# A delta-rule recurrence whose steps are split into single-engine operations and listed in one hand-made order, with the solved blocks on four column quarters

## Chip, cores, metric

One core of one Trainium2 chip runs the whole program in one launch. The metric is device time in microseconds (us), the median over executions. Matrix products run on TensorE (PE in the profile; its weight loads are PEld), elementwise work on VectorE (DVE), ScalarE (ACT) and GpSimd (POOL), and all transfers are issued by SyncE (SP). Every engine takes its own instructions strictly in the order in which the built program lists them, and waits on semaphores where an input is not there yet.

## What is computed

The program has three stages: a recurrence over 768 time steps for 4 x 8 = 32 heads of size 40, a mixture of attention experts, and a mixer with two pairs of dense layers. The change touches the first stage alone:

```python
for t in range(S):                       # S = 768
    y[:, :, t] = einsum('bhd,bhde->bhe', rt, state)
    Sa = einsum('bhde,bhe->bhd', state, at)
    state_decay = state * wt[:, :, None, :] - einsum('bhd,bhe->bhde', Sa, bt)
    state = state_decay + einsum('bhd,bhe->bhde', vt, kt)
x = moe2(moe(y))
```

## The kernel before

**Chunks and pairs.** The 768 steps are 12 chunks of 64 steps, and two chunks (128 steps) form a pair, of which there are 6. The 32 heads of 40 channels lie on partitions in 11 groups of three heads (120 rows; the last group has two). Three head ranges, `QUADS`, take 4, 4 and 3 groups, and are called q = 0, 1, 2 below: 12, 12 and 8 heads.

**What a pair needs ahead of its chunks.** Its inputs come by DMA: w, a and kb (k and b together) per pair, v, r and small strided copies of a and r (tiles `abd` and `rbd`, one buffer each) per chunk. `decay` makes running products of w on DVE, 31 dependent multiplications of 120x88, then four normalizing operations. `scale` multiplies a and kb by them. `scores` makes, per chunk, six masked products of kb and abd (PE, then DVE into tile `sc`), and copies 32x32 diagonal blocks of it to tile `td` (ACT). `solve` then inverts 128 x 32 small triangular systems on DVE: one transposition to `tp`, 31 steps of a product `pr` and a subtraction from `x`, and a transposition to `xt`. Each `x` needs the `pr` ahead of it, and each `pr` the `x` ahead of it.

**The chain of a chunk**, for each q: `z1` (state times a, PE), `tv` (scores times v and u, PE) and a copy to `zt` (ACT, with the sign turned), `xz` (the solved block `xt` times `zt`, PE), a copy to `vu` (ACT); then `tv` and `xz` again for the second 32 steps; `ds` (PE) and a product with `mf` into the new state `ST` (DVE); `st` transposes it to `S` (PE, ACT). The chunk's outputs follow at leisure: `vut`, `rs`, `hh`, `yy`. The first `xz` of a pair needs that pair's `xt`, so pair p cannot go on before `solve(p)` ended.

**Column halves.** `tv`, `xz`, `hh` and `yy` put two heads side by side into column halves of the PE array (`sides`): heads of groups g0 and g0+1 in one half, the others in the other, which makes 6 + 6 heads in q = 0 and 1, and 6 + 2 in q = 2. The copies of `zt` and `vu` take 32 partitions each: 240 columns twice, or 240 and 80 (`spans`).

**What sets the order.** Two strings, `EVEN` and `ODD`, name a chunk's operations in the order in which they are written, and `pump(1)` puts one step of the solve or of the decay (a list in the background, taken one by one) behind each. A scheduler of the framework then orders the instructions of every engine by its own model, and interleaves what it finds ready. The second and third stage are written after the recurrence and scheduled with it.

Of the kernel before, what the change touches and what calls it, by code (L numbers as in the profile page):

```python
# [31 lines left out]
FIRST = "p0 S p1 p2 k0 k1 k2 X L D M V q0 q1 q2"  # L32
SPIN = 28
PN = (1, 1)
EVEN = "m2 v0 h0 c0 z0 v1 c1 r0 c2 D v2 z2 x2 c3 m0 c4 x0 t2 z1 y0 x1 t1 c5 t0 h1 r1 r2 x3 y1 h2 c6 c7 k0 x5 c8 s0 c9 y2 x4 c10 c11 s2 d0 m1 S L d2 s1 k1 k2 d1"
ODD = "A z0 x0 v0 v1 z1 z2 r0 h0 x2 t0 m1 x1 m2 s0 v2 r1 y0 h1 m0 r2 M y1 p0 L p1 p2 h2 y2 x3 t1 t2 d0 s2 k0 x5 s1 k1 x4 d2 k2 d1"
QUADS = [(0, 4), (4, 8), (8, 11)]

def sides(q, n):

    g0, g1 = QUADS[q]
    a, b, e = n * g0, n * (g0 + 2), min(n * g1, 32 if n > 1 else G)
    for i in range(b - a):
# [26 lines left out]
class Rec:  # L70
# [39 lines left out]
    def load_w(s, p):  # L110
        w = s.ek.tile([120, G, 2, 64], F32, name="w", bufs=1)
        s.nc.sync.dma_start(w.rearrange("p g c t -> p g (c t)"), s.in_w[p])
        s.T[p] = dict(w=w)

    def load_a(s, p):
        a = s.wk.tile([120, G, 2, 64], F32, name="a")
        s.nc.sync.dma_start(a.rearrange("p g c t -> p g (c t)"), s.in_a[p])
        s.T[p]["a"] = a

    def load_kb(s, p):  # L120
        kb = s.ek.tile([120, G, 2, 128], F32, name="kb")
        s.nc.sync.dma_start(kb, s.in_kb[p].rearrange("p g c x t -> p g c (x t)"))
        s.T[p]["kb"] = kb
# [23 lines left out]
    def decay(s, p):  # L147
# [46 lines left out]
    def scores(s, c, u):  # L194

        nc, t = s.nc, s.T[c // 2]
        if u == 0:
            s.T["sc", c] = s.wk.tile([128, 32, 64], F32, name="sc", bufs=4)
        sc, abd = s.T["sc", c], s.T["abd", c]
        gs = range(2 * u, min(2 * u + 2, G))  # L200
        ps = s.ps.tile([128, 6, 64], F32, name="psc")
        n = 0
        for g in gs:
            k = 40 * nheads(g)
            nc.tensor.matmul(ps[:, n:n + nheads(g), :], t["kb"][:k, g, c % 2, :],  # L205
                             abd[:k, g, :nheads(g), :], start=True, stop=True)
            n += nheads(g)
        sv = sc[:, 6 * u:6 * u + n, :]
        m = s.mask[:, None, :].to_broadcast([128, n, 64])
        nc.vector.tensor_tensor(sv, ps[:, :n, :], m, OP.mult)  # L210
        if u == 5:

            if c % 2 == 0:
                s.T["td", c // 2] = s.ek.tile([128, 32, 32], F32, name="td", bufs=1)
            td = s.T["td", c // 2]
            for h in range(2):
                q = 64 * (1 - c % 2) + 32 * h
                nc.scalar.activation(td[q:q + 32],
                                     sc[q:q + 32, :, 32 * h:32 * h + 32], AF.Copy)

    def solve(s, p):
# [3 lines left out]
        yield  # L225
# [14 lines left out]
        s.solved = v.transpose(xt.rearrange("p s t -> p t s"), x)  # L240
        s.T["xt", p] = xt

    def kbt(s, c, q):
        nc, t = s.nc, s.T[c // 2]
        if q == 0:
            s.T["kbt", c] = s.wk.tile([128, 1280], F32, name="kbt")
# [3 lines left out]
        for g in range(g0, g1):  # L250
            k = 40 * nheads(g)
            nc.tensor.transpose(ps[:, o:o + k], t["kb"][:k, g, c % 2, :], s.ident[:k, :k])
            o += k
        nc.scalar.activation(s.T["kbt", c][:, 120 * g0:120 * g0 + o], ps[:, :o], AF.Copy)

    def ptt(s, p, q):
        nc, t = s.nc, s.T[p]
        if q == 0:
            s.T["ptt", p] = s.wk.tile([128, 1280], F32, name="ptt", bufs=3)
        g0, g1 = QUADS[q]  # L260
        ps = s.ps.tile([128, 512], F32, name="pm")
        o = 0
        for g in range(g0, g1):
            k = 40 * nheads(g)
            nc.tensor.transpose(ps[:, o:o + k], t["pt"][:k, g].rearrange("p c t -> p (c t)"), s.ident[:k, :k])
            o += k
        nc.scalar.activation(s.T["ptt", p][:, 120 * g0:120 * g0 + o], ps[:, :o], AF.Copy)


    def z1(s, c, q):  # L270
        nc, t = s.nc, s.T[c // 2]
        zu = s.pz.tile([128, 480], F32, name="zu")
        s.T["zu", q] = zu
        for g, b, i in sides(q, 1):
            k = 40 * nheads(g)
            nc.tensor.matmul(zu[64 * b:64 * b + 64, 120 * i:120 * i + k], t["a"][:k, g, c % 2, :],  # L276
                             s.ST[:k, g, :k], start=(i == 0), stop=False, skip_group_check=True)
        s.tv(c, q, 0)

    def tv(s, c, q, half):  # L280

        nc = s.nc
        zu, sc, vu = s.T["zu", q], s.T["sc", c], s.T["vu", c]
# [3 lines left out]
        for h, b, i in sides(q, 3):  # L287
# [864 lines left out]
```

## Time and profile before

| | us |
|---|---|
| median of 3 executions (1044.83 to 1048.39) | 1047.39 |
| the profiled execution, device time | 1045.46 |
| its span, first to last instruction | 1043.7 |
| PE busy (92%) | 959.1 |
| DVE busy (65%) | 674.4 |
| ACT busy (46%) | 479.3 |

The profile is of one execution. Busy time counts an instruction from its start to its end, and PE's overlap in its pipeline, so a busy PE can still lose time between two matmuls: the distance from start to start shows that. Other engines' instructions can overlap by a little as well. PEclk is the TensorE clock that was granted, as a share of 2.4 GHz. One f32 matmul of the program stands as two records in the trace.

### The profile page before, as it was taken

Reading aid. Unit: us, or ns where it says so; the run is one execution under the profiler, and the core shown is the slowest. Engines: PE = TensorE matmul, PEld = TensorE weight load, DVE = VectorE, ACT = ScalarE, POOL = GpSimd, SP = SyncE. Lnnn points to the kernel's source line nnn. Section 1 sums busy time; section 2 is a strip of 40 time slices with the busy share of each in tenths; the row PEclk is TensorE's granted clock in tenths of the full one; section 3 lists DMA queues with packets and bytes.
Section 4 is the critical chain, followed back from the end, with each engine's and each line's share of the span. In section 5 each row is a group of like instructions: output and inputs, shape, how many; then the busy total and the mean of one; then the engine's idle time right before and its main releaser. Section 6 shows DMA issues by size and latency. Waiting matters only on the chain.

```text
span 1043.7 us, 23515 instructions
## 1 busy us (share of the span) xinstructions
PE 959.1 (92%) x9313; PEld 823.1 (79%) x9313; DVE 674.4 (65%) x1793; ACT 479.3 (46%) x1250; POOL 167.7 (16%) x214
## 2 busy tenths in 40 slices
PE   2977997999999999966999999999998999999998
PEld 1646876888888898855877888888787898898987
DVE  6598898887989685747898777566287222222222
ACT  1324544656665665534677667666543121121211
POOL 5000000010000000352234132223255000000000
PEclk9977996999999999979999999999999999999999
DMA  8604422417253323455543441420262101101000
GB/s 172 138 1 96 100 67 74 111 41 170 53 123 74 86 61 117 157 165 145 154 116 99 118 115 31 96 65 26 87 205 63 56 1 56 39 18 57 1 26 26
DMA packets 101031, 88.84 MB, mean 85 GB/s; under 512 B 60785, under 2 KB 91073, under 8 KB 100321
## 3 DMA queue, kind: packets, MB, share of 16 engines
q1 hardware_dynamic: 100921, 87.34, 32.2%
q8 instruction: 74, 1.21, 0.5%
q14 instruction: 36, 0.29, 0.1%
HBM read 54.94 MB, written 15.73 MB: 68 GB/s over the span
## 4 chain that ended last, share of the span: by engine, by line
PE 66%; DVE 19%; DMA 6%; ACT 4%; issue 3%; POOL 1%; SPq 1%; DVEq 0%; ACTq 0%; POOLq 0%
PE pq L1045 12%; PE p L1059 11%; PE psc L205 4%; PE zu L289 3%; PE psc L387 3%; DVE pq L164 3%; PE po L872 3%; PE pq L846 3%; PE zu L302 2%; PE pq L998 2%; PE pm L325 2%; PE zu L276 2%; DVE x L237 2%; PE y L400 2%; DVE pr L235 2%
## 5 line engine op out<-in xcount | busy, mean ns | idle before, releaser
L1049 DVE SCALAR_TENSOR_TENSOR hl<-pq,hh 128x512 fp32r<-128x512 f32 x72 | 49.7, 690 | 153.6 <-ACT hh L1048 153.6
L1048 ACT ACTIVATE hh<-pq 128x512 fp32r<-128x512 f32 x72 | 42.9, 596 | 186.7 <-PE pq L1045 186.7
L1059 PE MATMUL p<-c2h,hh 128*128 128x320 f32 x288 | 90.8, 315 | 0.0
L819 ACT ACTIVATE a<-s,nm 128x512 f32<-128x512 f32 (+3 forms) x128 | 68.7, 542 | 46.4 <-DVE nm L816 21.6
L1059 PE MATMUL p<-c2l,hh 128*128 128x320 f32 x288 | 89.4, 311 | 0.2 <-POOL c2l L635 0.2
L1059 PE MATMUL p<-c2h,hl 128*128 128x320 f32 x288 | 89.5, 311 | 0.1
L306 ACT ACTIVATE vu<-zu 32x240 f32<-32x240 f32 (+1 forms) x144 | 48.8, 339 | 55.2 <-PE zu L302 45.1
L293 ACT ACTIVATE zt<-zu 32x240 f32<-32x240 f32 (+1 forms) x144 | 48.7, 338 | 51.7 <-PE zu L289 49.6
L814 DVE TENSOR_REDUCE nm<-s 128x1 f32<-128x512 f32 (+3 forms) x128 | 62.0, 500 | 15.7 <-PE s L813 10.8
L164 DVE TENSOR_TENSOR pq<-w,pq 120x88 f32<-120x88 f32 x186 | 61.2, 329 | 9.7 <-DMA w<-in_w 5.8
L832 POOL TENSOR_TENSOR a<-a,rs 128x128 f32<-128x128 f32 (+1 forms) x64 | 45.6, 734 | 126.6 <-DVE rs L827 84.5
L235 DVE TENSOR_TENSOR pr<-tp,x 128x31 f32<-128x31 f32 (+15 forms) x186 | 63.0, 339 | 3.8 <-DVE tp L226 0.5
L237 DVE TENSOR_TENSOR x<-x,pr 128x31 f32<-128x31 f32 (+15 forms) x186 | 63.2, 340 | 3.3
L289 PE MATMUL zu<-vu,sc 64*32 64x40 f32 (+1 forms) x1536 | 61.3, 220 | 1.2 <-ACT vu L306 1.2
L302 PE MATMUL zu<-zt,xt 64*32 64x40 f32 x1536 | 48.3, 211 | 12.5 <-DVE pq L161 6.8
L1045 PE MATMUL pq<-uh,c1h 128*128 128x512 f32 x144 | 57.6, 400 | 0.8 <-DVE ul L666 0.8
L289 PEld LDWEIGHTS zu<-vu,sc 64*32 64x32 f32 (+1 forms) x1536 | 53.2, 127 | 6.2 <-ACT vu L306 2.9
L1059 PEld LDWEIGHTS p<-c2h,hh 128*128 128x128 f32 x288 | 54.5, 189 | 3.7 <-DVE o L1062 1.2
L1045 PE MATMUL pq<-uh,c1l 128*128 128x512 f32 x144 | 57.1, 396 | 0.0
L1059 PEld LDWEIGHTS p<-c2l,hh 128*128 128x128 f32 x288 | 54.5, 189 | 2.9 <-POOL c2l L635 0.5
L387 PE MATMUL psc<-rbd,vut 120*128 120x192 f32 (+1 forms) x264 | 54.6, 341 | 1.9 <-DVE sr L391 1.6
L302 PEld LDWEIGHTS zu<-zt,xt 64*32 64x32 f32 x1536 | 40.3, 117 | 20.1 <-issue 12.8
(206 smaller groups left out, 2504.4 us busy)
## 6 DMA issues: line engine op xcount, KB each, us to landing
kb<-in_kb SPq DMA_DIRECT2D x5, 1320.0 KB
kh<-hb SPq DMA_DIRECT2D x64, 96.0 KB
cv<-in_c SPq DMA_DIRECT2D x18, 256.0 KB
w<-in_w SPq DMA_DIRECT2D x6, 660.0 KB
a<-in_a SPq DMA_DIRECT2D x6, 660.0 KB
r<-in_r SPq DMA_DIRECT2D x12, 330.0 KB
rbd<-in_r SPq DMA_DIRECT2D x36, 110.0 KB
vu<-in_v SPq DMA_DIRECT2D x12, 320.0 KB
```

Source lines behind the costliest of these rows:

```text
L164: e.tensor_tensor(two(pq, i + 1, x + 29 - 2 * i), two(t["w"], i, 31 - 2 * i), two(pq, i, x + 31 - 2 * i), OP.mult)
L235: v.tensor_tensor(prv, tp[:, j + 1:, j:j + 1].to_broadcast([128, n, j + 1]), x[:, j:j + 1, :j + 1].to_broadcast([128, n, j + 1]), OP.mult)
L237: v.tensor_tensor(x[:, j + 1:, :j + 1], x[:, j + 1:, :j + 1], prv, OP.subtract)
L289: nc.tensor.matmul(zu[o:o + m, 40 * i:40 * i + 40], sc[r, h, 32 * half:32 * half + m], vu[r, 40 * h:40 * h + 40], start=False, stop=True, ...
L302: nc.tensor.matmul(zu[o:o + 32, 240 + 40 * i:280 + 40 * i], xt[r, h, :], s.zt[half][r, 40 * h:40 * h + 40], start=True, stop=True, skip_gr ...
L306: nc.scalar.activation(vu[d:d + 32, o:o + n], zu[b + 32 * half:b + 32 * half + 32, 240:240 + n], AF.Copy)
L387: nc.tensor.matmul(ps[:, n:n + nheads(g), :], vt[:k, g - g0, :], rbd[:k, g, :nheads(g), :], start=True, stop=True)
L814: nc.vector.tensor_reduce(nm[:, x:x + 1], s, axis=AX.X, op=OP.max, negate=True)
L819: nc.scalar.activation(a[:, n0:n1], s, AF.Exp, bias=nm[:, -1:] if nb_ == 2 else nm[:, :1], accum_out=sm[:, x, i % 2:i % 2 + 1])
L1045: nc.tensor.matmul(p, l, r, start=(n == 0), stop=(n == 7))
L1049: nc.vector.scalar_tensor_tensor(hl, p, 0.0, hh, op0=OP.max, op1=OP.subtract)
L1059: nc.tensor.matmul(Y[s][i], hs[x][:, ts], w[:, k], start=(k + n == 0), stop=(k == 11 and n == 2))
```

## The change

Every operation of the recurrence is split into the part of one engine: lower-case letters of a list name a PE part or a DMA, capital letters the copy or product that empties it (`scores` and `scores_out`, `xz` and `xz_out`, and so on). Solve and decay are generators that yield after each single DVE instruction. Two lists, `HEAD` (up to the first `xt`) and `PAIR` (run once for each pair, with numbers relative to it), give the order, and `tc.manual_schedule` makes each engine keep it.

The solve works in `tp` itself, without `x`: 30 steps, each one column narrower, and -1 is written on the diagonal before the transposition, so that `xt` is the negative and the copy to `zt` needs no sign. `xz` puts its heads on four column quarters of 32, by contiguous quarters of the heads (3 each, or 2 in q = 2), with a place of its own for each half in the `zu` tile, and its copy is four pieces of 120 (or 80) columns. `sides`, `spans` and the new `blocks` split the heads evenly in all q: 6 + 6, 6 + 6, 4 + 4; group 9 of `z1` and `hh` becomes two matmuls for that.

```diff
+PAIR = """
+K-1.2 G0 N1.3 G0 G0 r-2.2.0 r-2.2.1 S-1.0 p1.2 F1 x-1.0.1 G0 P1.2 p1.0 j2 P1.0 R-2.2.1 p1.1 h-2.1 G0 y-2.1
...
+c3.0 Y-1.1 x0.0.0 R-1.2.0 E2 Z0.1 E2 E2 x0.2.0 S0.0 x0.1.0 C3.0 h-1.2 y-1.2 X0.0.0 X0.2.0 E2 c3.1 t0.0 C3.1 i0
...
+"""
...
+def sides(q):
+    g0, g1 = QUADS[q]
+    n = (min(3 * g1, 32) - 3 * g0) // 2
+    for i in range(n):
+        yield 3 * g0 + i, 0, i
+        yield 3 * g0 + n + i, 1, i
...
-        x = s.ek.tile([128, 32, 32], F32, name="x", bufs=1)
-        nc.gpsimd.memset(x, 0.0)
-        nc.gpsimd.memset(x.rearrange("p a b -> p (a b)")[:, ::33], 1.0)
-        for j in range(31):
+        for j in range(1, 31):
             n = 31 - j
             yield
             pr = s.ek.tile([128, 256], F32, name="pr")
-            prv = pr[:, :n * (j + 1)].rearrange("p (t c) -> p t c", c=j + 1)
-            v.tensor_tensor(prv, tp[:, j + 1:, j:j + 1].to_broadcast([128, n, j + 1]),
-                            x[:, j:j + 1, :j + 1].to_broadcast([128, n, j + 1]), OP.mult)
-            v.tensor_tensor(x[:, j + 1:, :j + 1], x[:, j + 1:, :j + 1], prv, OP.subtract)
+            prv = pr[:, :n * j].rearrange("p (t c) -> p t c", c=j)
+            v.tensor_tensor(prv, tp[:, j + 1:, j:j + 1].to_broadcast([128, n, j]),
+                            tp[:, j:j + 1, :j].to_broadcast([128, n, j]), OP.mult)
+            yield
+            v.tensor_tensor(tp[:, j + 1:, :j], tp[:, j + 1:, :j], prv, OP.subtract)
         yield
+        v.memset(tp.rearrange("p a b -> p (a b)")[:, ::33], -1.0)
...
-        for h, b, i in sides(q, 3):
-            o = 64 * b + 32 * half
-            nc.tensor.matmul(zu[o:o + 32, 240 + 40 * i:280 + 40 * i], xt[r, h, :],
-                             s.zt[half][r, 40 * h:40 * h + 40], start=True, stop=True, skip_group_check=True)
+        n = (min(3 * g1, 32) - 3 * g0) // 4
+        o = 240 + 120 * half
+        for i in range(n):
+            for b in range(4):
+                h = 3 * g0 + n * b + i
+                nc.tensor.matmul(zu[32 * b:32 * b + 32, o + 40 * i:o + 40 * i + 40], xt[r, h, :],
+                                 s.zt[half][r, 40 * h:40 * h + 40], start=False, stop=True, skip_group_check=True)
...
+        for b in range(4):
+            p = 40 * (3 * g0 + n * b)
+            nc.scalar.activation(vu[d:d + 32, p:p + 40 * n], zu[32 * b:32 * b + 32, o:o + 40 * n], AF.Copy)
...
+        with s.tc.manual_schedule(engines={E.PE, E.Activation, E.DVE, E.Pool, E.SP}):
+            for o in HEAD.split():
+                step(o, 0)
+            done.update(("E1", "G0"))
+            for i in range(s.np + 2):
+                for o in PAIR.split():
+                    step(o, i)
```

On DVE, before, these are the first steps of the solve of pair 0 and of pair 3 (L235 is `pr`, L237 `x`, L333 the product into `ST`, L226 the transposition from `td`):

```order
L226 STREAM_TRANSPOSE tp<-td 128x1024
L235 TENSOR_TENSOR pr<-tp,x 128x31
L237 TENSOR_TENSOR x<-x,pr 128x31
L235 TENSOR_TENSOR pr<-tp,x 128x60
L237 TENSOR_TENSOR x<-x,pr 128x30x2
L235 TENSOR_TENSOR pr<-tp,x 128x87
L237 TENSOR_TENSOR x<-x,pr 128x29x3
L235 TENSOR_TENSOR pr<-tp,x 128x112
L333 TENSOR_TENSOR ST<-pm,mf 120x480
L237 TENSOR_TENSOR x<-x,pr 128x28x4
```

And now, the first steps of the solve of pair 1 (L272 is the transposition, L278 `pr`, L281 the subtraction, L195 a decay step of pair 2, L246 a masked product, L395 the product into `ST`):

```order
L395 TENSOR_TENSOR ST<-pm,mf 120x480
L272 STREAM_TRANSPOSE tp<-td 128x1024
L278 TENSOR_TENSOR pr<-tp 128x30
L195 TENSOR_TENSOR pq<-w,pq 120x2x44
L281 TENSOR_TENSOR tp<-tp,pr 128x30
L278 TENSOR_TENSOR pr<-tp 128x58
L195 TENSOR_TENSOR pq<-w,pq 120x2x44
L281 TENSOR_TENSOR tp<-tp,pr 128x29x2
L195 TENSOR_TENSOR pq<-w,pq 120x2x44
L278 TENSOR_TENSOR pr<-tp 128x84
L281 TENSOR_TENSOR tp<-tp,pr 128x28x3
L246 TENSOR_TENSOR sr<-psc,mask 128x384
```

Between an instruction and the one that needs its result another stands now in most places. From the first transposition to the last `xt`, DVE has 791 instructions before and 788 now, and pairs of neighbours of which the second needs the first are 275 before and 157 now.

On PE, before, the stretch around the first `xz` of pair 3 reads so (L342 is `st`, L302 `xz`, L289 `tv`, L387 `rs`, L400 `yy`, L205 `scores`, L357 `hh`):

```order
L342 MATMUL pm<-ident,ST 120x120 x3
L302 MATMUL zu<-zt_113,xt 32x40 x21
L289 MATMUL zu<-vu,sc 32x40 x8
L302 MATMUL zu<-zt_113,xt 32x40 x11
L289 MATMUL zu<-vu,sc 32x40 x12
L387 MATMUL psc<-rbd,vut 128x192 x2
L289 MATMUL zu<-vu,sc 32x40 x12
L387 MATMUL psc<-rbd,vut 128x128
L302 MATMUL zu<-zt_114,xt 32x40 x12
L400 MATMUL y<-kbt,sr 64x40 x12
L205 MATMUL psc<-abd,kb 128x192 x4
L357 MATMUL y<-S,r 64x120
```

And now, at the same place of pairs 1 to 3 (L241 is `scores` and `rs`, L353 `xz`, L415 `hh`, L449 `yy`, L334 `tv`):

```order
L241 MATMUL psc<-abd,kb 128x192 x2
L353 MATMUL zu<-zt_113,xt 32x40 x32
L415 MATMUL y<-S,r 64x120
L415 MATMUL y<-S,r 64x80
L415 MATMUL y<-S,r 64x40
L415 MATMUL y<-S,r 64x80
L449 MATMUL y<-kbt,sr 64x40 x8
L241 MATMUL psc<-abd,kb 128x192 x2
L334 MATMUL zu<-vu,sc 32x40 x12
L241 MATMUL psc<-abd,kb 128x192 x4
L353 MATMUL zu<-zt_113,xt 32x40 x12
L241 MATMUL psc<-abd,kb 128x192 x2
```

An operation's matmuls stand together more often. Over the recurrence, neighbours on PE that use the array in different shapes (whole, column halves, or 64 rows by 32 columns) are 305 before and 183 now, and the matmuls are 3180 and 3193. In the two later stages the instructions are the same, but the scheduler lists some of them in another order: 1464 of 3442 PE instructions stand elsewhere.

On SP, in the list, the loads of a and kb of the next pair but one stand one behind the other, with the small copies `abd` behind them:

```order
L170 DMA r<-in_r 120x11x64
L151 DMA a<-in_a 120x1408
L156 DMA kb<-in_kb 120x2816
L234 DMA abd<-a 40x11x64 x3
L178 DMA rbd<-in_r 40x11x64 x3
```

The load of a waits for the last `z1` of the pair's odd chunk, and that of kb for its last turned kb (`kbt`), both on PE.

## Rows read from the trace of the kernel before

**Rows 1.** Windows: us, then busy time of each engine, clock, DMA share.

```profile
core 0: us, PE busy (x) PEld busy (x) DVE busy (x) ACT busy (x) POOL busy (x), PEclk, DMA share, GB/s
43.80:397.90 354.10, 324.12 (x4815) 275.14 (x4813) 306.52 (x791) 190.04 (x500) 17.93 (x29) 0.94 0.34 81
71.60:166.10 94.50, 78.82 (x1033) 67.17 (x1033) 86.23 (x233) 45.41 (x110) 4.58 (x10) 0.86 0.34 82
166.10:397.90 231.80, 224.13 (x3714) 198.56 (x3714) 195.16 (x497) 143.32 (x385) 13.35 (x19) 0.97 0.36 86
397.90:446.20 48.30, 45.88 (x831) 38.93 (x831) 29.23 (x61) 24.98 (x65) 13.59 (x10) 1.00 0.48 148
446.20:1043.70 597.50, 565.02 (x3527) 489.88 (x3527) 315.39 (x887) 251.82 (x662) 120.61 (x146) 0.98 0.28 77
```

**Rows 2.** Timeline of DVE: solves that begin and end, the last product into ST.

```profile
43.83 1.99 DVE L226 STREAM_TRANSPOSE tp<-td 128x1024 f32<-128x1024 f32 x1 [2.19 <-ACT td L218]
...
69.73 1.90 DVE L240 STREAM_TRANSPOSE xt<-x 128x1024 f32<-128x1024 f32 x1
...
395.97 1.96 DVE L240 STREAM_TRANSPOSE xt<-x 128x1024 f32<-128x1024 f32 x1
...
409.14 1.32 DVE L333 TENSOR_TENSOR ST<-pm,mf 120x480 f32<-120x480 f32 x3 [1.59 <-PE pm L327]
```

**Rows 3.** Waits between 43 and 440 us: total, times, longest.

```profile
DVE sr L391 <- PE psc L387: 17.0, 14, 5.1
```

**Rows 4.** Groups by shape, 30 to 430 us: busy, mean ns, idle before.

```profile
L164 DVE TENSOR_TENSOR pq<-w,pq 120x88 f32<-120x88 f32 x155 | 51.3, 331 | 2.8
...
L306 ACT ACTIVATE vu<-zu 32x240 f32<-32x240 f32 x117 | 42.2, 360 | 54.2 <-PE zu L302 44.4 <-issue 8.3
...
L306 ACT ACTIVATE vu<-zu 32x80 f32<-32x80 f32 x23 | 5.3, 229 | 0.3
...
L237 DVE TENSOR_TENSOR x<-x,pr 128x255 f32<-128x255 f32 x12 | 5.0, 416 | 0.1
...
L237 DVE TENSOR_TENSOR x<-x,pr 128x31 f32<-128x31 f32 x12 | 2.4, 200 | 0.3
```

**Rows 5.** Timeline of DVE: solve steps by themselves, then with others between.

```profile
46.57 0.21 DVE L237 TENSOR_TENSOR x<-x,pr 128x31 f32<-128x31 f32 x1
46.81 0.22 DVE L235 TENSOR_TENSOR pr<-tp,x 128x60 f32<-128x60 f32 x1
...
127.76 0.33 DVE L164 TENSOR_TENSOR pq<-w,pq 120x88 f32<-120x88 f32 x1
128.00 0.25 DVE L237 TENSOR_TENSOR x<-x,pr 128x87 f32<-128x87 f32 x1
```

**Rows 6.** Timeline of PE: groups in one array shape, and at a change.

```profile
184.19 0.85 PE L289 MATMUL zu<-vu,sc 128*64 128x40 f32 x24
184.86 0.50 PE L276 MATMUL zu<-ST,a 120*64 120x120 f32 x5
...
195.46 0.62 PE L302 MATMUL zu<-zt,xt 64*32 64x40 f32 x24
195.91 1.02 PE L289 MATMUL zu<-vu,sc 64*32 64x40 f32 x40
...
242.94 0.62 PE L302 MATMUL zu<-zt,xt 64*32 64x40 f32 x24
243.50 0.65 PE L367 MATMUL pm<-ident,vu 128*120 128x128 f32 x4
```

**Rows 7.** Timelines of SP and DVE: loads of kb, a, and their use.

```profile
179.40 0.33 SPq L122 DMA_DIRECT2D kb<-in_kb  x1
185.50 0.34 SPq L117 DMA_DIRECT2D a<-in_a  x1
...
188.32 1.63 DVE L186 TENSOR_TENSOR kb<-kb,pq 120x1408 f32<-120x1408 f32 x1 [2.35 <-DMA kb<-in_kb]
...
191.42 1.62 DVE L182 TENSOR_TENSOR a<-a,pq 120x1408 f32<-120x1408 f32 x1 [0.21 <-issue]
```

More of the change, by code (lines that the diff above doesn't have):

```diff
@@ L192, in abd_load, with product @@
             nc.sync.dma_start(abd[40 * h:40 * h + 40, :, h, :], a[40 * h:40 * h + 40, :, c % 2, :])
[L194 to L200, printed above, removed]
+    def product(s, w, mov, gs):
         ps = s.ps.tile([128, 6, 64], F32, name="psc")
@@ new lines, in xz_out, with mf @@
+    def xz_out(s, c, q, half):
+        nc, zu, vu = s.nc, s.T["zu", c, q], s.T["vu", c]
+        g0, g1 = QUADS[q]
+        n = (min(3 * g1, 32) - 3 * g0) // 4
+        o = 240 + 120 * half
+        d = 64 * (1 - c % 2) + 32 * half
+        for b in range(4):
+            p = 40 * (3 * g0 + n * b)
+            nc.scalar.activation(vu[d:d + 32, p:p + 40 * n], zu[32 * b:32 * b + 32, o:o + 40 * n], AF.Copy)
+    def mf(s, c, q):
+        g0, g1 = QUADS[q]
+        f = s.T[(c + 1) // 2]["f"][:, (c + 1) % 2]
+        s.T["mf", c, q] = mf = s.wk.tile([120, 4, 120], F32, name="mf", bufs=3)
+        for g in range(g0, g1):
+            s.nc.scalar.activation(mf[:, g - g0], s.bdm, AF.Copy, scale=f[:, g:g + 1])
@@ L432, in first @@
         s.consts()
-        s.bg = [s.decay(0)]
-        s.pump(1000)
+        for _ in s.decay(0):
+            pass
+        for i in range(4):
+            s.norm(0, i)
+        s.decayed(0)
         t = s.T[0]
@@ L448, in first, with advance @@
                 s.scores(c, u)
+                s.scores_out(c, u)
+            s.blocks_out(c)
+    def advance(s, f, p):
+        if (f, p) not in s.T:
+            s.T[f, p] = f(p)
+        next(s.T[f, p])
     def run(s):
-        n = s.np
         s.first()
-        def loads():
-            s.load_w(1)
-            s.load_a(1)
-            s.load_kb(1)
-        def all(f):
-            for _ in f:
-                pass
-        def decay():
-            with s.tc.issue_after(s.solved.ins):
-                all(s.decay(1))
@@ L467, in run @@
-        do = dict(S=lambda: all(s.solve(0)), p=lambda q: s.ptt(0, q), L=loads, D=decay,
-                  M=lambda: s.scale(1), q=lambda q: s.ptt(1, q), V=lambda: s.load_chunk(1),
-                  k=lambda q: s.kbt(0, q), X=lambda: s.spin(s.T['sc', 1], SPIN))
-        for o in FIRST.split():
-            if n > 1 or o[0] not in "LDMq":
-                do[o[0]](*map(int, o[1:]))
-        s.bg = []
-        for c in range(2 * n):
-            s.chunk(c)
+        by_pair = dict(W=s.load_w, I=s.load_a, J=s.load_kb, E=lambda p: s.advance(s.decay, p), N=s.norm, F=s.decayed,
+                       A=s.scale_a, B=s.scale_kb, G=lambda p: s.advance(s.solve, p), p=s.ptt, P=s.ptt_out, O=s.store,
+                       a=lambda p: s.spin(s.T["sc", 1], SPIN))
@@ new lines, in run, with step @@
+        done = set(HEAD_DONE.split())
+        skip = {f"{k}{2 * s.np - 1}.{q}" for k in "mdD" for q in range(3)} | {f"{k}0.{q}" for k in "sS" for q in range(3)}
+        def step(o, i):
+            k, (x, *rest) = o[0], map(int, o[1:].split("."))
+            one = k in by_pair
+            x += i if one else 2 * i
+            if k in "EG" and f"{k}{x}" in done:
+                return
+            name = ".".join([f"{k}{x}", *map(str, rest)])
+            if 0 <= x < (s.np if one else 2 * s.np) and name not in done and name not in skip:
+                (by_pair if one else by_chunk)[k](x, *rest)
+                if k not in "EG":
+                    done.add(name)
```

374 lines of the change are left out of this document (159 added, 215 removed).

## The prediction, made before the result was known

> **What bounds the kernel now.** I first cut the span by the solves, since a pair cannot go on before its `xt`. The first transposition starts at 43.83 us, the first `xt` ends at 71.6 and the last at 397.9 [rows 2]; the recurrence ends at 446.2, and the two later stages take 597.5 [rows 1]. So 354.1 us lie between the first solve's start and the last one's end, and there two engines are near their limit at once: PE is busy for 324.1 and DVE for 306.5, while ACT has 190.0 [rows 1]. The reader should see how unevenly the time goes: from the first `xt` to the second it takes 94.5 us at a granted clock of 0.86 of 2.4 GHz, and the other four pairs take 231.8, or 58.0 each [rows 1]. In those four PE is idle for 7.7 us and DVE for 36.6. DVE's idle time over all of the 354.1 is 47.6. The view of waits shows what it mostly is: DVE has a masked product to make and PE has not delivered it (17.0 us in 14 waits) [rows 3]. DVE is late, PE then waits for the solve, and later DVE waits for PE: each loses time that the other lacks. After the last `xt` it takes 48.3 us to the end of the recurrence [rows 1].
>
> **DVE's work.** One instruction of the solve takes 0.200 us with 31 columns and 0.416 with 255 [rows 4], so 0.170 plus 0.00096 a column. A solve had 31 steps of two instructions and 5456 columns each way; now it has 30 steps and 4960. That is 992 columns and two instructions less, 0.95 + 0.34 = 1.3 us a pair. The new write of the diagonal has no row; it has 32 columns, and the shortest solve instruction, with 31, is 0.200, so it costs between 0 and 0.2, and I take 0.1, a middle, since it only writes. Six solves save 7.2.
>
> The order saves more. Where the next instruction needs the result, it starts after the end: `x` takes 0.21 and the next `pr` starts 0.24 behind its start. Where it does not, it starts earlier than the end: a decay step takes 0.33 and the solve step behind it starts after 0.24 [rows 5]. That is 0.03 of a gap against 0.09 of overlap. The order lists 275 neighbours of the first kind before and 157 now, so 118 change kind: 10.6 us less busy time, and the gaps shrink from 275 x 0.03 = 8.3 to 4.7. Not every independent neighbour overlaps, above all where PSUM is read, so this is an upper bound; the lower one is nothing, and I take it whole, because the 118 are nearly all solve and decay steps, whose rows these are. DVE then needs 306.5 - 7.2 - 10.6 + 4.7 = 293.4 us from the first transposition to the last `xt`.
>
> In this the decay of pair 1 (31 x 0.331 = 10.3 [rows 4]), its normalizing and its scaling (3 x 1.62 [rows 7]) move from behind the first `xt` to within the first solve. They fill the solve's gaps: of 17 or so, 38 neighbours give back 0.12 each and the 38 new instructions overlap by 0.09, so the first `xt` comes some 8 us later, near 79, and what stood behind it is gone from the next 94.5 us.
>
> **PE's work.** In the four later pairs PE has 224.1 / 4 = 56.0 us of work each [rows 1]. Three things make it less:
> - Changes of the array's shape. The 24 records of an `xz` take 0.45 us to the next start where the next group has the same shape (195.46 to 195.91), and 0.56 where it has not (242.94 to 243.50) [rows 6]: 0.11 a change. 122 fewer changes are 13.4 us in all, 2.2 a pair.
> - `xz` on quarters. Those 24 records are 12 heads on two halves, 37.5 ns for each two. In q = 2 one half held six heads, so it took 12 x 37.5 ns = 0.45 too, and a half-chunk 1.35. If four quarters run as two halves do, it takes 0.225 + 0.225 + 0.15 = 0.60; if only two ever run at once, 0.45 + 0.45 + 0.30 = 1.20. Over 24 half-chunks this saves 18.0 or 3.6. No row shows four at once; I take 18.0, because the rows show two as independent of each other.
> - Even halves in q = 2. `tv`'s first half takes 0.67 for 24 records on two halves [rows 6], 56 ns for each two; two heads of two records less on the long side are 0.22, the same for `yy`, and 2 x 2 x 37.5 ns = 0.15 for `tv`'s second half. 0.59 a chunk, 7.1 in all. The one matmul more in `z1` and `hh` balances columns in the same way, and I set it at nothing: 160 columns on a side instead of 240 and 80.
>
> PE needs 56.0 - 2.2 - 3.0 - 1.2 = 49.6 us a pair, against DVE's 293.4 less some 35 for the first solve, over five pairs: 51.7. DVE leads, narrowly.
>
> **ACT.** The copies of `vu` become four pieces. With 0.360 for 240 columns and 0.229 for 80 [rows 4], 120 columns take 0.262: 1.05 in place of 0.72 for a set, 72 sets, 24 us more. ACT has 164 us to spare in the 354.1, and the pieces of one q lie beside PE's products for the next, so I count nothing; if that cover were gone it would be the 24.
>
> **What DVE still waits for.** From the end of an `xt`, the chain of `xz`, `tv`, `xz` and `ds` brings the first product into `ST` 11.2 us later (397.9 to 409.14 [rows 2]); the list puts that product ahead of the next solve, with about 25 instructions between, at a mean of 306.5 / 791 = 0.39 less overlap some 9 us. 1 to 2.5 us are left, 1.8 x 4 = 7. The loads: a was in use 5.9 us after its issue (185.50 to 191.42) and kb 8.9 us (179.40 to 188.32, DVE had waited 2.35) [rows 7]. The list issues both together behind the odd chunk's `z1`, some 5 us ahead of a's use: 1 a pair, 4. At the start one `abd` buffer has to be loaded again between the two chunks' scores, and the first `xz` stands behind it on PE: 4.5. For PE and DVE so near each other I add 3. Sum 18.5, against 47.6 - 8.3 = 39.3 before.
>
> **The sum.** Last `xt` at 43.8 + 293.4 + 18.5 = 355.7. The tail was 48.3; two chunks save 2 x (0.59 + 1.5) = 4.2, so 44.1. The recurrence ends at 399.8 in place of 446.2, 46.4 earlier. The later stages keep their instructions; some are listed in another order, which I bound by a third of PE's 32.5 us of idle time there [rows 1], 10 either way, and take at nothing. The profiled execution's 1045.46 becomes 999.1; the median before is 1.9 above it, so I predict **1001 us**.
>
> **The rivals.**
> - *Quarters do not run four at once.* PE needs 2.4 more a pair, 52.0, and is level with DVE; the chain behind `xt` grows by 0.5. Up to 14.4 come back, of which I count 9: 1010. For it: nothing in the rows shows four. Against: two halves share the same 64 rows already, at no loss. The Trainium skill (TensorE: Matmul & The Clock Gate, Wait — 56ns, not 53.3ns?) gives about 25 ns as the least distance from one matmul's start to the next, which would forbid any gain; this trace is already below it, 0.45 us / 24 = 19 ns a record [rows 6].
> - *The waits stay.* The list was fixed ahead, as the scheduler's was, and neither engine can leave its order when the other is late. If DVE waits 39.3 as before, the last `xt` is at 376.5 and the program at 1022. For it: both engines would be within 5% of their limit. Against: the large waits before come with `EVEN`, which asks for the next pair's scores only late in a chunk.
> - *The copies lie on the path.* The 24 us of ACT come back: 1025. For it: the second `tv` and `ds` need these copies. Against: ACT is idle for nearly half of the stretch [rows 1]. The Trainium skill (TensorEngine Tiling (Array Packing), PSUM Bottleneck) says that packing speeds up TensorE and not the emptying of PSUM, which may become the bottleneck behind it; no row here shows ACT as one.
> - *No change*: the waits come to 65 us, 13 a pair, 1047.
> - *Slower: the loads.* a, kb and behind them `abd` go one after the other on SP's queue. If kb lands some 15 us late, as it would if both loads took twice the 14.8 us of the rows, every solve step and score behind the scaling is late by that, 12 net of cover, in five pairs: 60 more, 1061. It decides from 46.4 / 5 = 9.3 us a pair. Against: the DMA queues are busy for a third of the time [rows 1], and kb waited only 2.35 here.
>
> **How the numbers follow.** The forecast has a chance of 0.55 and its own range is 987 to 1014: the later stages' 10 either way, and waits from 14 to 22. Quarters without effect 0.15, waits as before 0.18, copies 0.04, no change 0.04, loads 0.04. 0.3% is about what a measurement of this kernel can tell from no change. The time is lower by more than that in the first four cases, 0.92. For 8 in 10 the range takes in the second and third case with their own spread: 982 to 1030.
>
> **What would show it.** Last `xt` near 356 and the first near 79; the time from one `xt` to the next near 55 in the middle pairs and no first one of 94.5; DVE's busy time from the first transposition to the last `xt` near 289; an `xz` group of 24 records at about 0.23 us to the next of its shape. It is wrong if DVE's waits for PE stay near 40 us, if those 24 records still take 0.45, or if `a` and `kb` become DVE's largest wait.

## The result, and the profile after

The changed kernel takes 992.24 us, the median of four executions (988.11 to 998.65), against 1046.2 for the kernel before in the same series: a ratio of 0.9488 with a 95% interval of 0.9429 to 0.9546. It is faster, by 54 us where 46 were forecast. In a later series it took 991.83 (0.9487, 0.9458 to 0.9516). The profiled execution took 988.11, with a span of 986.4. (Of one experiment below, the arithmetic without the order, some executions were disturbed; its ratio leaves them out.)

The same windows as in [rows 1], cut at the first transposition, the first and the last `xt` and the end of the recurrence:

```profile
40.80:76.20 35.40, 26.12 (x97) 13.45 (x95) 34.53 (x103) 4.41 (x12) 1.55 (x3) 0.90 0.10 23
76.20:140.00 63.80, 60.38 (x1019) 53.83 (x1019) 56.82 (x158) 45.67 (x131) 2.65 (x4) 0.95 0.46 95
140.00:346.80 206.80, 202.56 (x3829) 181.05 (x3829) 195.12 (x529) 161.65 (x487) 9.17 (x13) 1.00 0.47 105
40.80:346.80 306.00, 289.06 (x4944) 248.33 (x4943) 286.47 (x788) 211.73 (x630) 13.37 (x20) 0.98 0.43 94
346.80:391.00 44.20, 39.88 (x807) 35.14 (x805) 31.04 (x59) 29.23 (x92) 14.56 (x11) 0.92 0.57 169
391.00:986.40 595.40, 566.55 (x3527) 492.14 (x3527) 313.04 (x887) 250.94 (x659) 119.59 (x145) 0.97 0.27 77
```

The stretch from the first transposition to the last `xt` fell from 354.1 to 306.0 us. That is 48.1 of the 57.3 between the two spans; 3.0 lie ahead of it, 4.1 in the tail, 2.1 in the later stages. DVE's busy time in the stretch fell by 20.0 (306.5 to 286.5) and its idle time by 28.1 (47.6 to 19.5). By place, the part up to the second `xt` fell from 122.3 us (43.8 to 166.1) to 99.2 and the four intervals behind it from 231.8 to 206.8: 23.1 and 25.0 us. The reader should also see the third row: in the last four intervals PE is busy for 202.6 of 206.8 us and DVE for 195.1, so both are near their limit. DVE was busy there for 195.2 before as well; what is gone is its idle time, 36.6 us then and 11.7 now.

DVE's timeline, as in [rows 2], and its waits in the stretch (total, times, longest), as in [rows 3]:

```profile
40.81 1.99 DVE L272 STREAM_TRANSPOSE tp<-td 128x1024 f32<-128x1024 f32 x1 [2.19 <-ACT td L266]
...
74.30 1.93 DVE L285 STREAM_TRANSPOSE xt<-tp 128x1024 f32<-128x1024 f32 x1
...
344.84 2.00 DVE L285 STREAM_TRANSPOSE xt<-tp 128x1024 f32<-128x1024 f32 x1
...
355.08 0.66 DVE L395 TENSOR_TENSOR ST<-pm,mf 120x480 f32<-120x480 f32 x1 [1.17 <-PE pm L383]
```

```profile
DVE sc L246 <- PE psc L241: 8.9, 13, 1.3
DVE tp L272 <- ACT td L266: 2.2, 1, 2.2
DVE ST L395 <- PE pm L383: 1.6, 2, 1.1
DVE sr L246 <- PE psc L241: 1.3, 2, 1.1
DVE ptt L456 <- PE y L449: 0.2, 1, 0.2
```

For comparison, DVE's waits for PE before, within the same stretch (43.8 to 397.9 us):

```profile
DVE sc L210 <- PE psc L205: 9.0, 16, 2.3
DVE sr L391 <- PE psc L387: 8.6, 9, 3.0
DVE ST L333 <- PE pm L327: 7.2, 6, 3.6
DVE ptt L404 <- PE y L400: 4.3, 10, 0.9
```

These four were 29.1 us and are 12.0 now (the 2.2 for `tp` lie ahead of the first transposition, outside the stretch); the wait for `sr` went from 8.6 to 1.3. (The 17.0 for `sr` in [rows 3] runs on to 440 us, beyond the last `xt`.) The chain from the end of an `xt` to the first product into `ST` takes 8.2 us (346.84 to 355.08) where it took 11.2.

PE's timeline, as in [rows 6]: an `xz` ahead of a group of another shape, and one ahead of its own shape.

```profile
155.94 0.42 PE L353 MATMUL zu<-zt,xt 64*32 64x40 f32 x24
156.28 0.90 PE L449 MATMUL y<-kbt,sr 128*64 128x40 f32 x24
...
160.00 0.58 PE L353 MATMUL zu<-zt,xt 64*32 64x40 f32 x40
160.39 0.62 PE L334 MATMUL zu<-vu,sc 64*32 64x40 f32 x24
```

40 records take 0.39 us to the next start, 9.75 ns each, where 24 on halves took 0.45, 18.8 each. Four quarters do run at once. 24 records ahead of another shape take 0.34, by this 0.23 and 0.11 for the change of shape. The four copies on ACT, by shape in the stretch, as in [rows 4]:

```profile
L364 ACT ACTIVATE vu<-zu 32x120 f32<-32x120 f32 x160 | 41.8, 261 | 8.5 <-PE zu L353 5.8
...
L364 ACT ACTIVATE vu<-zu 32x80 f32<-32x80 f32 x80 | 18.2, 228 | 6.0 <-PE zu L353 4.9
```

### The profile page after: what moved, and what is told of

Read it like the earlier page. It is cut to its first block, busy times and chain, and to the rows that moved or that the text cites. A ratio compares the mean times of both kernels' runs of the same rounds, so it can differ in the third digit from the quotient of the medians.

```text
span 986.4 us, 23682 instructions
## 1 busy us (share of the span) xinstructions
PE 914.2 (93%) x9350; PEld 790.6 (80%) x9350; DVE 653.8 (66%) x1787; ACT 500.5 (51%) x1390; POOL 161.0 (16%) x202
## 4 chain that ended last, share of the span: by engine, by line
PE 64%; DVE 22%; DMA 5%; ACT 4%; issue 3%; SPq 1%; POOL 0%; DVEq 0%; ACTq 0%; POOLq 0%
PE pq L1023 12%; PE p L1037 12%; PE psc L241 8%; PE po L850 4%; DVE pq L195 3%; PE pq L824 3%; DVE pr L278 2%; DVE tp L281 2%; PE pq L989 2%; PE pq L976 2%; PE pq L752 2%; PE s L788 2%; PE pq L865 2%; PE zu L334 2%; PE y L449 2%
## 5 line engine op out<-in xcount | busy, mean ns | idle before, releaser
L364 ACT ACTIVATE vu<-zu 32x120 f32<-32x120 f32 (+1 forms) x288 | 72.0, 250 | 17.2 <-PE zu L353 12.7
L195 DVE TENSOR_TENSOR pq<-w,pq 120x88 f32<-120x88 f32 x186 | 61.1, 329 | 8.0 <-DMA w<-in_w 5.6
L241 PE MATMUL psc<-abd,kb 120*128 120x192 f32 (+1 forms) x242 | 53.9, 364 | 7.2 <-DMA abd<-a 3.8
L281 DVE TENSOR_TENSOR tp<-tp,pr 128x30 f32<-128x30 f32 (+9 forms) x180 | 58.6, 326 | 2.1
L278 DVE TENSOR_TENSOR pr<-tp 128x30 f32<-128x30 f32 (+9 forms) x180 | 58.5, 325 | 1.8
L1023 PE MATMUL pq<-uh,c1h 128*128 128x512 f32 x144 | 57.1, 396 | 0.8 <-DVE ul L644 0.8
L341 ACT ACTIVATE zt<-zu 32x240 f32<-32x240 f32 (+1 forms) x144 | 49.0, 340 | 14.4 <-PE zu L334 12.3
L1037 PEld LDWEIGHTS p<-c2h,hl 128*128 128x128 f32 x288 | 54.5, 189 | 0.3 <-DVE hl L1027 0.3
L241 PE MATMUL psc<-rbd,vut 120*128 120x192 f32 (+1 forms) x264 | 53.5, 333 | 0.0
L241 PEld LDWEIGHTS psc<-abd,kb 120*128 120x128 f32 (+1 forms) x242 | 42.5, 208 | 12.7 <-DVE kb L228 3.4
L824 PE MATMUL pq<-ident,a 128*128 128x128 f32 x336 | 50.4, 276 | 1.4 <-DVE kz L762 0.6
```

Source lines behind the costliest of these rows:

```text
L241: s.nc.tensor.matmul(ps[:, n:n + nheads(g), :], w(g)[:k], mov[:k, g, :nheads(g), :], start=True, stop=True)
L281: v.tensor_tensor(tp[:, j + 1:, :j], tp[:, j + 1:, :j], prv, OP.subtract)
L364: nc.scalar.activation(vu[d:d + 32, p:p + 40 * n], zu[32 * b:32 * b + 32, o:o + 40 * n], AF.Copy)
L824: nc.tensor.transpose(p[:, o:o + 128], es[i][:, 128 * (j0 + j):128 * (j0 + j) + 128], ident)
L1023: nc.tensor.matmul(p, l, r, start=(n == 0), stop=(n == 7))
L1037: nc.tensor.matmul(Y[s][i], hs[x][:, ts], w[:, k], start=(k + n == 0), stop=(k == 11 and n == 2))
```

## The experiments

My theory was the prediction's: DVE and PE are both near their limit, the list lets neither wait, and each edit then counts. The first rivals were that the arithmetic alone does it, or the order alone. Each figure is a median in its own series, with the ratio to the kernel before in that series and its 95% interval. The diffs are against the changed kernel unless said otherwise.

**The order without the arithmetic.** The solve goes back into a tile `x`, `xz` onto two halves with two copies, q = 2 to 6 + 2 heads:

```diff
-        for j in range(1, 31):
+        for j in range(31):
...
-        for i in range(n):
-            for b in range(4):
...
+        for h, b, i in sides(q):
...
-    n = (min(3 * g1, 32) - 3 * g0) // 2
+    n, e = 6, min(3 * g1, 32) - 3 * g0
```

> The changed kernel with its lists and split operations, but the old arithmetic: the solve in a tile of its own with 31 steps, xz on two column halves with two copies, and 6 + 2 last heads. My theory (DVE and PE are level, so work given back to either shows): DVE gets 7.2 us more, PE about 21 in five pairs and 4 in the tail, ACT 24 less; the last xt comes near 365 and the whole takes 1010 to 1018, so the order alone is worth some 30 us. Rival, the order is nearly the whole gain: 1000 or less. Rival, the arithmetic carries it: 1030 or more.

Measured 1010.99 us (0.9687, 0.9658 to 0.9716); the last `xt` ended at 365.2. As expected: the order alone is worth some 33 us.

**The arithmetic without the order.** The same three edits the other way round, put into the kernel before:

```diff
-        for j in range(31):
+        for j in range(1, 31):
...
-        for h, b, i in sides(q, 3):
-            o = 64 * b + 32 * half
...
+        for i in range(n):
+            for b in range(4):
+                h = 3 * g0 + n * b + i
```

> The kernel before with its own order, but the new arithmetic: the solve in place, xz on four quarters with four copies, 4 + 4 last heads. My theory: DVE saves 7.2 us and PE up to 25, but the large waits of DVE for PE's products come with the old lists and mostly stay (over 25 us of DVE waits between the first transposition and the last xt), so 1020 to 1035. Rival, the arithmetic carries the gain: 1005 or less, with DVE waits near 15. Rival, the old order hides it all: within 5 us of the kernel before.

Measured: a ratio of 0.9998 (0.9955 to 1.0042), so no gain. My 1020 to 1035 was too good, and the rival "the old order hides it all" holds. The ratio is over executions of 1035.48 to 1047.67; the profiled one was the quickest, at a mean granted clock of 0.962, the others at 0.952 to 0.954. Even there the stretch is no more than 3.9 us shorter than before. Its window, and DVE's largest waits:

```profile
39.50:389.70 350.20, 313.47 (x4835) 261.10 (x4833) 295.89 (x783) 209.32 (x618) 12.32 (x19) 0.92 0.34 81
```

```profile
DVE ST L348 <- PE pm L342: 15.9, 11, 6.3
DVE sc L223 <- PE psc L218: 12.2, 17, 4.1
DVE sr L406 <- PE psc L402: 6.0, 13, 1.8
```

DVE is busy 10.6 us less than before and PE 10.7, but DVE is idle for 54.3 instead of 47.6 and PE for 36.7 instead of 30.0: of what either engine saves, 6.7 us go into its own idle time, and DVE's three largest waits, 34.1 us, are all for PE.

**The list given to the scheduler.**

```diff
-        with s.tc.manual_schedule(engines={E.PE, E.Activation, E.DVE, E.Pool, E.SP}):
+        with nullcontext():
```

> The changed kernel with the same split operations written in the same order, but each engine's order left to the framework's scheduler, as in the kernel before: 229 changes of the array's shape instead of 183, and 265 solve and decay neighbours that need each other instead of 166. My theory (the list itself is worth most of what the arithmetic alone did not give): DVE's waits for PE come back, 20 to 40 us, with 12 for the neighbours and 5 for the shapes: 1015 to 1045. Rival, splitting the operations is what helps and the scheduler does as well with them: within 8 us of the changed kernel.

Measured 1026.13 us (0.9796, 0.9742 to 0.9849), some 34 more than with the list. Two rows show it:

```profile
0.00:53.90 53.90, 27.73 (x173) 21.91 (x174) 39.42 (x95) 13.37 (x27) 15.04 (x30) 0.84 0.71 144
53.90:381.40 327.50, 298.86 (x4847) 255.92 (x4845) 281.82 (x750) 208.91 (x614) 11.99 (x17) 0.94 0.37 85
```

The scheduler puts pair 1's decay, normalizing and scaling ahead of the first solve, whose transposition starts 13 us later, at 53.9; and in the stretch DVE is idle for 45.7 us, as before. Of the 34 us I had foreseen the second part alone. Split operations and the new arithmetic together, without the fixed order, are worth some 18 us (1.5 to 2.6% by the interval).

**Neighbours that need each other.**

```diff
             v.tensor_tensor(prv, tp[:, j + 1:, j:j + 1].to_broadcast([128, n, j]),
                             tp[:, j:j + 1, :j].to_broadcast([128, n, j]), OP.mult)
-            yield
             v.tensor_tensor(tp[:, j + 1:, :j], tp[:, j + 1:, :j], prv, OP.subtract)
+            yield
```

> The changed kernel with each subtraction of the solve listed right behind its product, so that 128 more neighbours on DVE need each other's result; no instruction is added. My theory: 0.12 us each, 15 us more DVE time in the stretch from the first transposition to the last xt, and since DVE and PE are level most of it shows: 1000 to 1007. Rival, PE alone sets the time now: within 4 us of the changed kernel, and DVE's waits for PE shrink. Rival, list order of neighbours costs nothing: DVE's gaps behind the solve's instructions are the same.

Measured 1009.17 us (0.9640, 0.9591 to 0.9690), 17 more, with not one instruction added. The stretch, and three neighbours on DVE:

```profile
39.60:362.90 323.30, 291.47 (x4944) 250.15 (x4943) 297.68 (x788) 211.73 (x630) 14.31 (x20) 0.97 0.40 89
```

```profile
106.55 0.30 DVE L278 TENSOR_TENSOR pr<-tp 128x150 f32<-128x150 f32 x1
106.88 0.32 DVE L280 TENSOR_TENSOR tp<-tp,pr 128x150 f32<-128x150 f32 x1
107.11 0.33 DVE L195 TENSOR_TENSOR pq<-w,pq 120x88 f32<-120x88 f32 x1
```

The subtraction starts 0.33 us behind a product of 0.30; the decay step, which needs neither, 0.23 behind a subtraction of 0.32. The stretch grew by 17.3 us, 0.135 for each of the 128 pairs, a little over the 0.12 that I took.

**The old solve; `xz` on halves; twice as many copies.** Two parts of the run with the order alone, each undone by itself in the changed kernel; and, in the third run, the copies cut in two:

```diff
-            nc.scalar.activation(vu[d:d + 32, p:p + 40 * n], zu[32 * b:32 * b + 32, o:o + 40 * n], AF.Copy)
+            for z in (0, 20 * n):
+                nc.scalar.activation(vu[d:d + 32, p + z:p + z + 20 * n],
+                                     zu[32 * b:32 * b + 32, o + z:o + z + 20 * n], AF.Copy)
```

> The changed kernel with the old solve: a tile x of its own, 31 steps each one column wider, listed at the same places. My theory: 1.2 to 1.3 us more a solve on DVE, 7 us in all, of which 5 to 8 show: 997 to 1000. Rival, PE alone sets the time: within 2 us of the changed kernel.

> The changed kernel with one part undone: xz on two column halves again, copied in two pieces, everything else and the order kept. My theory (four quarters run at once, and PE is level with DVE): an xz group of 24 records takes 0.45 us again, PE gets 14 to 18 us more work, and the time is 8 to 15 us longer, 1000 to 1007. Rival, DVE alone sets the time and PE has slack: within 4 us of the changed kernel, and PE's idle time shrinks by the 14 to 18. Rival, the four copies lay on the path: faster than the changed kernel by 5 or more.

> The changed kernel with each of the 288 copies to vu cut into two of half the columns, so that ACT has 288 instructions and about 45 us more. My theory (ACT's copies lie beside PE's other products): at most 6 us longer, 992 to 998. Rival, the copies lie on the path: 15 to 45 us longer, 1007 to 1037, and PE's and DVE's waits for ACT appear in the view of waits.

Measured 999.14 us (0.9548, 0.9492 to 0.9605), 998.98 (0.9590, 0.9556 to 0.9624) and 992.24 (0.9506, 0.9484 to 0.9529). The stretches of the first two:

```profile
40.30:356.50 316.20, 294.20 (x4945) 251.49 (x4944) 293.54 (x794) 211.81 (x630) 18.93 (x30) 0.96 0.41 91
```

```profile
40.30:350.90 310.60, 295.75 (x4947) 257.96 (x4945) 287.06 (x788) 193.87 (x510) 13.37 (x20) 0.98 0.42 92
```

The old solve makes DVE 7.1 us busier and the stretch 10.2 longer. In the last four intervals alone it is 4.6 us busier (199.7) and they are 4.2 longer (211.0), so nearly all of it shows. Halves give 4.6 in the stretch and 3.3 in the tail (47.5 against 44.2), some 7 in all, where I had expected 8 to 15. By the records, halves with 4 + 4 heads are an estimated 24 x (2 x (0.45 - 0.234) + 0.30 - 0.156) = 13.8 us more PE work, so about half of it is hidden. The doubled copies cost nothing that can be measured. That test was weaker than meant: the two halves of a piece overlap, and ACT was busy for 12.3 us more in the stretch (72.8 for the copies instead of 60.0), not 45.

**Which engine leads.** To take work from DVE, the decay of pairs 1 to 5 goes to GpSimd; in the second run the last two normalizing multiplications and the scaling of kb too.

```diff
-        t["pq"], e = pq, nc.vector
+        t["pq"], e = pq, nc.gpsimd if p else nc.vector
...
+            e = s.nc.gpsimd if p else e
...
-        s.nc.vector.tensor_tensor(kbx, kbx, s.T[p]["qt"], OP.mult)
+        s.nc.gpsimd.tensor_tensor(kbx, kbx, s.T[p]["qt"], OP.mult)
```

> The changed kernel itself, on the same chip as the three that go with it: 988 to 996, since its executions so far lie between 988.11 and 998.65. My theory has nothing else to say of it. If its profile shows the first transposition near 40 and the last xt near 346 again, the marks of one profile can be compared between kernels to about 1 us.

> The changed kernel with the 31 decay multiplications of pairs 1 to 5 on GpSimd instead of DVE, at the same places of the lists. By GpSimd's rows one should take about 0.35 us there (0.21 with 11 columns, 0.41 with 128). DVE loses 155 instructions, but 91 more solve neighbours need each other's result, so it saves about 29 us and not 51. My theory since the runs before (DVE leads, PE has some 10 us of slack in the stretch up to the last xt): that slack is what can be gained, 978 to 986, with PE's waits for DVE gone and DVE's waits for PE doubled. Rival, PE already sets the time: within 4 us of the changed kernel. Rival, GpSimd's work slows DVE's instructions down: the solve's mean rises above 0.33 us and the time is over 996.

> As the run with the decay on GpSimd, and the last two normalizing multiplications and both scalings of kb of pairs 1 to 5 there too: 23 us more off DVE, but kb is scaled some 3 us later in each pair (2.7 instead of 1.6 us for each of two). My theory: PE sets the time by then and waits for kb, so no better than the run with the decay alone, from 3 us faster to 8 us slower than it. Rival, DVE still leads: 10 us or more faster than it.

Measured 991.83 us for the changed kernel (its last `xt` at 348.3; a mark moves by 2 us between executions), 989.61 with the decay moved (0.9468, 0.9442 to 0.9493) and 1006.21 with more moved (0.9620, 0.9590 to 0.9650). The last four intervals of the run with the decay moved, and DVE's longest wait in its whole stretch (39.5 to 345.0 us):

```profile
138.90:345.00 206.10, 200.88 (x3830) 181.05 (x3829) 181.89 (x443) 161.73 (x487) 47.59 (x87) 1.00 0.47 105
```

```profile
DVE sc L246 <- PE psc L241: 24.3, 22, 4.8
```

DVE has 13.2 us less to do there, and the four intervals take 206.1 us instead of 206.8. My 978 to 986 is wrong; the time is that of the rival "PE already sets the time", and the 2 us are within the intervals. Whether that rival's reason holds, the windows say. A solve (from its transposition to the end of its `xt`) and the time from there to the next transposition, first in the changed kernel, then with the decay moved:

```profile
149.70:194.50 44.80, 43.05 (x751) 38.57 (x749) 43.79 (x122) 33.63 (x100) 2.65 (x4) 1.00 0.58 125
194.50:204.20 9.70, 9.57 (x219) 8.18 (x218) 9.09 (x26) 7.81 (x24) 0.00 (x0) 1.00 0.22 61
```

```profile
148.40:193.40 45.00, 42.63 (x755) 38.58 (x751) 43.16 (x103) 33.86 (x101) 13.57 (x26) 1.00 0.55 121
193.40:202.80 9.40, 9.28 (x217) 8.05 (x218) 5.44 (x12) 7.52 (x23) 5.65 (x10) 1.00 0.26 73
```

Between two solves PE is busy nearly all the time, and DVE's 3.6 us less there, three times, are 10.8 of the 13.2. They could only become waiting: in the four intervals DVE's waits for scores rise from 3.7 to 10.8 us. Within the solves DVE lost 19 instructions but only 0.6 us of busy time, since the solve's products and subtractions became slower (below) and overlap less, and it stayed the busier engine. So the run shows that PE sets the time between the solves; within them it took too little from DVE to show anything. The same windows with the old solve (the solve only) and with `xz` on halves:

```profile
155.30:200.90 45.60, 43.56 (x751) 38.60 (x749) 44.77 (x124) 33.60 (x100) 1.49 (x3) 1.00 0.56 123
```

```profile
150.50:195.60 45.10, 43.86 (x751) 39.82 (x749) 43.84 (x122) 31.23 (x84) 2.65 (x4) 1.00 0.60 124
195.60:205.60 10.00, 10.00 (x219) 8.82 (x218) 9.19 (x25) 6.52 (x16) 0.00 (x0) 1.00 0.21 56
```

One us more on DVE makes this solve 0.8 us longer (the next two, with 1.1 more, 1.2 and 1.3), 0.8 more on PE makes it 0.3 longer, and 0.4 more on PE between two solves makes that time 0.3 longer. DVE leads in the solves, PE between them. The third run shows another price. The group of the solve's products in the changed kernel's stretch, and below it in this run, with GpSimd's scaling:

```profile
L278 DVE TENSOR_TENSOR pr<-tp 128x30 f32<-128x30 f32 (+9 forms) x180 | 58.5, 325 | 1.8
```

```profile
L279 DVE TENSOR_TENSOR pr<-tp 128x30 f32<-128x30 f32 (+9 forms) x180 | 79.7, 443 | 3.7
...
L229 POOL TENSOR_TENSOR kb<-kb,pq 120x1408 f32<-120x1408 f32 x10 | 33.6, 3375 | 26.5 <-DMA kb<-in_kb 19.8 <-PE pm L426 6.6
```

The solve's products take 443 ns in the mean instead of 325 in the run in which GpSimd does more beside them (353 with the decay alone there). Of its products and subtractions, counted in the trace, the 112 that run while a GpSimd instruction runs take 686 ns in the mean, the other 248 take 331. The Trainium skill (SBUF — State Buffer, Who interferes with whom) says that a DVE instruction with two SBUF inputs contends with a GpSimd instruction that reads SBUF; the traces agree. The first window above is 47.1 us long in this run, with DVE busy for 45.5:

```profile
155.50:202.60 47.10, 43.26 (x755) 38.64 (x751) 45.54 (x99) 33.86 (x101) 25.52 (x35) 1.00 0.54 116
```

How much of the 14 us is this, and how much the later scaling of kb, no run separates.

**Filling products.** PE stands still from 61.4 to 68.7 us in the changed kernel, and its granted clock falls, to 0.50 (1.2 GHz) from 68 to 72. (From 72 to 76 it is back at 0.93, so it is not low all the way to 84, as I had put it.)

```diff
-SPIN = 28
+SPIN = 44
```

A second run has 37.

> The changed kernel with 44 instead of 28 filling products on PE in the first solve, which would end near 68 us instead of 61. In the changed kernel's profile PE then stands still until 68.7, and the granted clock is 0.5 to 0.7 from 64 to 84 us, where the scores take 0.34 us a record and DVE waits for them. My theory: at the full clock this work takes half, and 3 to 6 us are gained: 986 to 989, with the second transposition 3 to 6 us earlier than 95.6. Rival, the clock falls anyway, at the next wait: within 2 us of the changed kernel.

> The changed kernel with 37 filling products on PE, which end near 68 us, just ahead of the transpositions that wait for the decay, where 44 ended at 73.8 and pushed those back by 5. My theory: the granted clock stays at 1.0 until 82, the scores of the second pair take half as long, and the second transposition comes 1 to 3 us earlier after the first one than the 54.8 of the changed kernel. Rival, the clock falls at PE's next stop and takes the gain back, as with 44: 54.8 or more.

Measured 997.69 us (0.9529, 0.9479 to 0.9579) and 993.06 (0.9500, 0.9475 to 0.9526): no gain. The second transposition comes 58.2 and 54.9 us behind the first, where the changed kernel's two profiles have 54.8 and 57.1. The changed kernel's windows, then those with 37:

```profile
64.00:68.00 4.00, 0.00 (x0) 0.00 (x0) 3.96 (x16) 0.00 (x0) 1.55 (x3) 0.71 0.00 0
68.00:72.00 4.00, 3.28 (x23) 2.90 (x25) 3.93 (x7) 1.87 (x4) 0.00 (x0) 0.50 0.04 8
```

```profile
68.00:72.00 4.00, 2.68 (x44) 2.18 (x43) 3.93 (x7) 3.38 (x10) 0.00 (x0) 1.00 0.16 36
72.00:76.00 4.00, 2.11 (x7) 1.42 (x8) 3.97 (x6) 1.00 (x3) 0.00 (x0) 0.80 0.89 205
76.00:80.00 4.00, 4.00 (x14) 4.00 (x14) 1.28 (x4) 0.00 (x0) 0.00 (x0) 0.50 0.07 13
```

With 37 the first fall of the clock, to 0.50, is put off. But from 72 to 76 us PE waits for the scaling of kb, and the clock falls then, just when the scores run for which DVE waits. With 44 the clock stays at 1.00 from 60 to 86 us and those scores run at the full clock. But PE comes to its own work at 73.6 instead of 68.7, and behind its next wait, of 2.6 us for a decay step, the clock falls after all. Its windows, and the last of these in the changed kernel's second profile:

```profile
76.00:80.00 4.00, 4.00 (x35) 3.31 (x32) 2.17 (x5) 2.67 (x9) 0.00 (x0) 1.00 0.04 7
88.00:90.00 2.00, 2.00 (x28) 1.47 (x27) 1.11 (x3) 1.24 (x6) 0.00 (x0) 0.50 1.12 187
```

```profile
88.00:90.00 2.00, 2.00 (x28) 1.49 (x26) 0.80 (x2) 0.91 (x4) 0.00 (x0) 0.50 1.12 172
```

In the changed kernel's first profile the clock is 1.00 there, which goes with its 54.8 against 57.1. So in both runs the rival's reason holds, that the clock falls at a later wait; with 44 the time is 5 us above the rival's "within 2 us". None of these versions beats the changed kernel measurably.

## Why the prediction was right, and where it was not

| | forecast | measured |
|---|---|---|
| first `xt` (us) | 79 | 76.2 |
| first transposition to last `xt` | 311.9 | 306.0 |
| DVE busy in it | 289 | 286.5 |
| DVE idle in it | 23 | 19.5 |
| last `xt` | 355.7 | 346.8 |
| tail | 44.1 | 44.2 |
| recurrence end | 399.8 | 391.0 |
| later stages | 597.5 | 595.4 |

The profiled execution came out 11.0 us below the 999.1: 3.0 at the head, 5.9 in the stretch, 2.1 in the later stages.

- **The head.** I kept its 43.8 us, and it is 40.8. The new order is not needed for that: the old one with the new arithmetic starts its first solve at 39.5. It is also why the first `xt` came at 76.2: from the first transposition it took 35.4 us, as forecast (79 - 43.8 = 35.2).
- **The intervals.** From one `xt` to the next it takes 54.5, 54.1 and 52.6 us in the middle pairs, where I had said 55, and 63.8 in the first one instead of 94.5. That pair 1's decay and scaling now run within the first solve fits this, but no run undoes it by itself.
- **DVE's work.** Solve, neighbours and overlaps were sized right: 286.5 of 289 us busy. Undoing the solve's part cost 7 us, and 128 more dependent neighbours cost 17, so both terms are on the path.
- **DVE's waits** were the mis-sized term: 18.5 forecast, 12.0 measured, all of them for PE. The 4.5 for the reload of `abd` was a wait of PE (2.1 us), and the 4 for a and kb did not come: DVE has no wait for a load. So the slower rival, the loads, had nothing to stand on. The short gaps between neighbours are the other 7.5 of DVE's idle time, where the sum had 4.7, so that the total came within 4 us is partly luck. The prediction also read the 17.0 us for `sr` as most of the stretch's idle time; in the stretch it was 8.6 of 47.6, and only all four waits for PE together, 29.1, are most of it.
- **"DVE leads, narrowly"** is right within the solves and not outside them. In the solve shown above DVE is busy for 43.8 of 44.8 us and waits 0.3 us for PE, and work added to DVE shows nearly whole. From an `xt` to the next transposition PE is busy for 9.6 of 9.7 us, and in the last solve and its `xt` (310.8 to 346.8) for 35.9 of 36.0. PE had 50.6 us of work a pair in the last four, where I had put 49.6. That 206.8 / 4 = 51.7 is the figure that I had for DVE is luck: over the five pairs DVE is busy for (286.5 - 34.5) / 5 = 50.4.
- **Quarters** run four at once, as taken. The size on the path was off: of 13.8 us about half is hidden. **The changes of shape**, 13.4 us of PE in the sum, were not undone by themselves: 0.11 us for one is measured, their worth on the path is not.
- **The copies** are off the path, as counted, as far as the weak test goes.
- **The tail and the later stages** came as forecast, to 0.1 and 2.1 us.
- **What I had not said:** the parts do not add. The order alone gives 33 us, the arithmetic alone nothing, both together 53.

## What to carry to other kernels

Where two engines hand work to each other and both are near their limit, less work on either can end as waiting for the other: here the arithmetic gave nothing in the old order and 20 us in the new one. So look for an order first. Ask which engine leads in each stretch and not over the whole: DVE led in the solves and PE between them. When an engine is relieved, look where its busy time fell: 10.8 of 13.2 us fell where the other engine had no time to spare. On an in-order engine put an independent instruction between two that need each other: 0.135 us a pair here, without changing a single operation.

## What the runs showed of the hardware

- Copies on ACT overlap only in part. With the pieces cut in two, the second half starts some 90 ns before the first ends, and the next piece, read from other partitions, some 13 ns behind the end: 480 copies of 203 and 187 ns were busy for 72.8 us. The uncut pieces of the changed kernel do not overlap: 160 of 261 ns were busy for 41.8 us, 275 ns from start to start.
- GpSimd's decay step took 510 ns beside DVE's work, where its rows by size pointed to some 350, and its scaling of kb 3375 where I expected 2700. Both sides pay: offloading from DVE to GpSimd slowed the solve's products by 9% (353 ns) to 36% (443 ns).
